# Linear attention and a top-2 mixture of experts on one core: nine tokens a partition for two batches at a time, row-tiled attention matmuls, all of attention and dispatch ahead of the experts

## The chip, the cores and the metric

One core of a Trainium2 chip. The metric is the device time of one execution in microseconds (us), lower is better. Before the change: 599.88 us, median of 3 runs (597.19 to 603.38). Profiles are of single executions; their spans lie 2 us below the times. The runs fell on several chips; they are called by their numbers (9, 14, 11, 5), and the two traces made first, of the kernel before and of the changed one, are "the traces on record".

## The reference, cut to what matters

```python
# q, k, v: (8 batches, 8 heads, 576 tokens, 64); phi(x) = elu(x) + 1
kv  = einsum('bhsd,bhse->bhde', phi(k), v);  z = sum(phi(k), axis=2)
num = einsum('bhsd,bhde->bhse', phi(q), kv); den = phi(q) . z + 1e-6
x   = (num / den), heads side by side                       # (4608 tokens, 512)
noisy = x @ w_gate + log1p(exp(x @ w_noise)) * noise        # (4608, 8)
top2, softmax over the two
for e in range(8):                                          # w1: (8, 512, 1024), w2: (8, 1024, 512)
    for k in range(2):
        out[mask] += top2_w[mask, k] * (relu(x[mask] @ w1[e]) @ w2[e])
```

## The kernel before

Attention runs in four groups of two batches. A group makes kv, then num (which carries the router's logits along in extra columns), then the routing, then 18 indirect scatters ("a dispatch") that put each token's row, with its id and gate, into the list of its expert in DRAM. An expert then takes 1280 rows in three chunks (512, 512, 256): two matmuls, and for each 128 rows a scatter of y into the output. Since a token has two experts, the second one gathers what the first wrote (L), adds and scatters. All of these transfers are issued by GpSimd (POOL), and so are q, k, v and the weights, which are cast on the way; only x, the expert's sorted rows, is loaded by SyncE, transposed on the way.

```python
# load: 4 tokens a partition for 512 tokens of a batch; the last 64 tokens of each batch apart
nc.gpsimd.dma_start(out=kt[:], in_=main(self.k, b))                       # rows of 512 B in bf16
nc.gpsimd.dma_start(out=km[64*j:64*j+64], in_=self.k[b, :, 512:S, :]...)  # rows of 128 B
...
# kv, per batch: 4 full matmuls and one of 64 rows for each pair of heads
for ci in range(4):
    nc.tensor.matmul(out=ps[:, i, 0:192], lhsT=phk[:, hp, ci, :], rhs=vt[:, hp::4, 64*ci:64*ci+64], ...)
nc.tensor.matmul(out=ps[:, i, 0:192], lhsT=phkm[po:po+64, hp, 0, :], rhs=vm[po:po+64, hp::4, :], ...)
...
# experts: weights three ahead, ten gathers at once, x in four buffers
for e in range(E):
    for n in (512, 512, 256):
        xt = self.xp.tile(...)                       # pool of 4
        nc.sync.dma_start(out=xt, in_=x_sorted rows, transpose=True)
        hT = self.mm1(w1, xt, n)
        flush(prev)                                  # mm2, y, scatter of the chunk before
        if t0 == 0:
            if e + 3 < E: self.load_w(e + 3)
            for t in range(T_CAP): L[t] = self.gather(gi[:, t:t+1]) if e > 0 else None
```

Of the kernel before, what the change touches and what calls it, by code (L numbers as in the profile page):

```python
# [15 lines left out]
P = 128  # L16
# [6 lines left out]
NG = 4  # L23
NC = 9
T_CAP = 10
CAP = T_CAP * P
REGION = N_TOK
ROW_W = HD + 16
BIG = 1.0e6
KVW = 162  # L30

# [6 lines left out]
def build_constants(ctx, tc, consts, w_gate, w_noise, noise):  # L38
    nc = tc.nc
    c = {}  # L40

# [19 lines left out]

    c8 = consts.tile([P, E], FP32, name="c8")
    nc.gpsimd.iota(c8[:], pattern=[[-1, E]], base=E, channel_multiplier=0,
                   allow_small_or_imprecise_dtypes=True)
    c["c8"] = c8

    tokid = consts.tile([P, NC], FP32, name="tokid")
    nc.gpsimd.iota(tokid[:, 0:8], pattern=[[S, 2], [1, 4]], base=0, channel_multiplier=4,
                   allow_small_or_imprecise_dtypes=True)
    for half in range(2):  # L70
        nc.gpsimd.iota(tokid[64 * half : 64 * half + 64, 8:9], pattern=[[0, 1]],
                       base=512 + S * half, channel_multiplier=1,
                       allow_small_or_imprecise_dtypes=True)
# [14 lines left out]

    wst = consts.tile([P, 4, 16], FP32, name="wst")
# [11 lines left out]

    noise_sb = consts.tile([P, NG, NC, E], FP32, name="noise_sb")
    for b in range(B):
        g, j = divmod(b, 2)
        nc.scalar.dma_start(
            out=noise_sb[:, g, 4 * j : 4 * j + 4, :],
            in_=noise[b * S : b * S + 512, :].rearrange("(p c) e -> p (c e)", c=4),
        )
    for j in range(2):
        src = noise[512 + j * S : 512 + j * S + 64, :]  # L110
        src = bass.AP(tensor=src.tensor, offset=src.offset,
                      ap=[src.ap[0], [2 * S * E, NG], [1, E]])
        nc.scalar.dma_start(out=noise_sb[64 * j : 64 * j + 64, :, 8, :], in_=src)
# [4 lines left out]
    c["carry"] = carry  # L118
    return c


class PhaseA:
    def __init__(self, ctx, tc, q, k, v, x_sorted, c):
        self.tc, self.nc, self.c = tc, tc.nc, c
        self.q, self.k, self.v, self.x_sorted = q, k, v, x_sorted
        nc = tc.nc
        pool = lambda name, bufs, **kw: ctx.enter_context(tc.tile_pool(name=name, bufs=bufs, **kw))
        self.ld = pool("A_ld", 3)
        self.mx = pool("A_mx", 2)
        self.pers = pool("A_pers", 1)  # L130
        self.tmp = pool("A_tmp", 2)
        self.php = pool("A_php", 2)
        self.kvp = pool("A_kvp", 3)
        self.pq = pool("A_pq", 3)
        self.rt = pool("A_rt", 2)
        self.ps_kv = pool("A_ps_kv", 2, space=PSUM)
        self.ps_t = pool("A_ps_t", 2, space=PSUM)
        self.ps_num = pool("A_ps_num", 2, space=PSUM)
        self.vt = []
        for i in range(4):  # L140
            t = self.pers.tile([P, 12, 256], BF16, name=f"v{i}")
            nc.vector.memset(t[:, 8:12, :], 1.0)
            self.vt.append(t)
        self.vm = []
        for i in range(2):
            t = self.pers.tile([P, 12, D], BF16, name=f"vm{i}")
            nc.vector.memset(t[:, 8:12, :], 1.0)
            self.vm.append(t)
        self.xrow = []
        for i in range(2):  # L150
            t = self.pers.tile([P, NC, ROW_W], BF16, name=f"xrow{i}")
            nc.vector.memset(t[:, :, HD:ROW_W], 0.0)
            self.xrow.append(t)

    def load(self, g):
        nc = self.nc
        st = {"g": g, "k": [], "q": [], "v": []}
        km = self.mx.tile([P, 8, D], BF16, name="km")
        qm = self.mx.tile([P, 8, D], BF16, name="qm")
        vm = self.vm[g % 2]  # L160
        main = lambda t, b: t[b, :, 0:512, :].rearrange("h (p c) d -> p h (c d)", c=4)
        for j in range(2):
            b = 2 * g + j
            kt = self.ld.tile([P, 8, 256], BF16, name="kt")
            qt = self.ld.tile([P, 8, 256], BF16, name="qt")
            vt = self.vt[b % 4]
            nc.gpsimd.dma_start(out=kt[:], in_=main(self.k, b))
            nc.gpsimd.dma_start(out=km[64 * j : 64 * j + 64], in_=self.k[b, :, 512:S, :].rearrange("h p d -> p h d"))
            nc.gpsimd.dma_start(out=vt[:, 0:8, :], in_=main(self.v, b))
            nc.gpsimd.dma_start(out=vm[64 * j : 64 * j + 64, 0:8, :], in_=self.v[b, :, 512:S, :].rearrange("h p d -> p h d"))  # L170
            nc.gpsimd.dma_start(out=qt[:], in_=main(self.q, b))
            nc.gpsimd.dma_start(out=qm[64 * j : 64 * j + 64], in_=self.q[b, :, 512:S, :].rearrange("h p d -> p h d"))
            st["k"].append(kt); st["q"].append(qt); st["v"].append(vt)
        st["km"], st["qm"], st["vm"] = km, qm, vm
        return st

    def phi(self, src, nc_, name):

        nc = self.nc
        n = 512 * nc_  # L180
        flat = src[:].rearrange("p a b -> p (a b)")
        e = self.tmp.tile([P, n], BF16, name=f"e{nc_}")
        t = self.tmp.tile([P, n], BF16, name=f"t{nc_}")
        r = self.php.tile([P, 4, nc_, P], BF16, name=name)
        nc.scalar.activation(out=e[:], in_=flat, func=ACT.Exp)  # L185
        nc.vector.tensor_scalar(out=t[:], in0=flat, scalar1=0.0, scalar2=1.0, op0=ALU.max, op1=ALU.add)
        half = n // 2
        for two in range(2):
            v = lambda x: x[:, half * two : half * two + half].rearrange("p (h c d) -> p h c d", h=4, d=D)
            nc.vector.tensor_tensor(out=r[:, :, :, 64 * two : 64 * two + 64], in0=v(e), in1=v(t), op=ALU.min)  # L190
        return r

    def kv(self, st, j, phk, phkm):
        nc, c = self.nc, self.c
        kvbd = self.kvp.tile([P, 4, KVW], BF16, name="kvbd")
        vt, vm = st["v"][j], st["vm"]
        po = 64 * j
        for half in range(2):
            ps = self.ps_kv.tile([P, 2, 256], FP32, name="kv_ps")
            for i in range(2):  # L200
                hp = 2 * half + i
                for ci in range(4):
                    nc.tensor.matmul(  # L203
                        out=ps[:, i, 0:192],
                        lhsT=phk[:, hp, ci, :],
                        rhs=vt[:, hp::4, 64 * ci : 64 * ci + 64],
                        start=(i == 0 and ci == 0), stop=False, skip_group_check=True,
                    )
                nc.tensor.matmul(
                    out=ps[:, i, 0:192],  # L210
                    lhsT=phkm[po : po + 64, hp, 0, :],
                    rhs=vm[po : po + 64, hp::4, :],
                    start=False, stop=(i == 1), skip_group_check=True,
                )
            nc.vector.tensor_tensor(
                out=kvbd[:, 2 * half : 2 * half + 2, 0:130],
                in0=ps[:, :, 0:130],
                in1=_ap(c["mask"], [[0, 2], [1, 130]]),
                op=ALU.mult,
            )  # L220
        tp = self.ps_t.tile([P, 1024], BF16, name="t_ps")
        for hp in range(4):
            nc.tensor.transpose(tp[:, hp * P : hp * P + P], kvbd[:, hp, 0:128], c["ident"][:])
        kvt = self.kvp.tile([P, 512], BF16, name="kvt")
        nc.scalar.copy(out=kvt[:], in_=tp[:, 0:512])
        wp = self.ps_kv.tile([P, 2, 256], FP32, name="kv_ps")
        wpv = wp[:].rearrange("p a b -> p (a b)")[:, 0:128].rearrange("p (a b) -> p a b", a=4)
        for hp in range(4):
            nc.tensor.matmul(
                out=wpv[:, hp, :], lhsT=kvt[:, hp * P : hp * P + P], rhs=c["wblk"][:, hp, :],  # L230
                start=(hp == 0), stop=(hp == 3), skip_group_check=True,
            )
        nc.vector.tensor_copy(out=kvbd[:, :, 130:162], in_=wpv)
        return kvbd

    def q_t(self, phq):

        nc, c = self.nc, self.c
        pqt = self.pq.tile([P, 4, 512], BF16, name="pqt")
        for half in range(2):  # L240
            tp = self.ps_t.tile([P, 1024], BF16, name="t_ps")
            for i in range(2):
# [8 lines left out]
    def q_tm(self, phqm):  # L251
# [3 lines left out]
        for hp in range(4):  # L255
            nc.tensor.transpose(tp[:, hp * P : hp * P + P], phqm[:, hp, 0, :], c["ident"][:])
# [127 lines left out]
    def run(self):  # L384
        nxt = self.load(0)
        for g in range(NG):
            st = nxt
            if g + 1 < NG:
                nxt = self.load(g + 1)
# [242 lines left out]
```

## Time and profile before

Time 599.88 us, span of the profile 595.4. Milestones, read from the timelines of POOL and TensorE:

| milestone of the kernel before | us |
|---|---|
| matmuls that make the ranks of the four groups (a token's place in its expert's list) | 71.9, 127.4, 171.3, 218.3 |
| last dispatch issued | 243.7 |
| last dispatch landed, first x asked for | 246.0 |
| end | 595.4 |

Read it as four stretches: up to the end of dispatch, from there to the first gather (expert 0, which has none), six periods from one expert's first gather to the next, and the rest. The prediction below shows the lines, and gives the starts of the dispatches and the first gathers.

### The profile page before, as it was taken

What the parts mean: (1) busy time and instruction counts of PE and PEld (TensorE: products, weight loads), DVE (VectorE), ACT (ScalarE), POOL (GpSimd) and SP (SyncE); (2) the same over time, 40 slices, a digit from 0 to 9 for tenths busy, and PEclk for the clock granted to TensorE, in tenths of its full rate; (3) what the DMA queues carried; (4) which work ended last, traced back from release to release, by engine and by line L of the source; (5) the groups of instructions that cost most, each with busy time, mean ns of one, the idle gap of its engine ahead of it and who ended that gap; (6) DMA issues with size and microseconds to landing.
All of it is one profiled execution on the core that took longest, in us unless ns stands there. A gap on an engine that the chain in (4) does not pass through costs nothing. (4 is left out here: it accounts for less than half of the span.)

```text
span 595.4 us, 5833 instructions
## 1 busy us (share of the span) xinstructions
PE 373.5 (63%) x1976; PEld 194.5 (33%) x1976; DVE 221.8 (37%) x638; ACT 170.2 (29%) x265; POOL 288.7 (48%) x315
## 2 busy tenths in 40 slices
PE   0173173137245300199989928969948968989984
PEld 0151142015124100045444404425424434444442
DVE  4359655375650560413233104314304304333122
ACT  0466444025021120062333401421511321423410
POOL 6445378427427117204346516725706726565364
PEclk9996555556555555589999978998987998998998
DMA  9999954995602002555864993993893995573153
GB/s 168 210 191 191 191 131 101 192 209 157 124 27 102 36 10 106 128 91 130 184 101 121 184 110 80 228 140 101 217 120 101 243 146 145 189 157 145 57 160 128
DMA packets 122985, 82.65 MB, mean 139 GB/s; under 512 B 74164, under 2 KB 108980, under 8 KB 122944
## 3 DMA queue, kind: packets, MB, share of 16 engines
q0 software_dynamic: 65888, 69.02, 56.8%
q1 hardware_dynamic: 54272, 12.98, 14.8%
q10 hardware_dynamic: 2784, 0.18, 0.4%
q8 instruction: 17, 0.28, 0.2%
q14 instruction: 24, 0.20, 0.1%
HBM read 80.72 MB, written 32.87 MB: 191 GB/s over the span
## 5 line engine op out<-in xcount | busy, mean ns | idle before, releaser
L474 PE MATMUL h_ps<-xt,w 128*128 128x512 bf16 (+1 forms) x768 | 150.5, 355 | 39.5 <-DMA xt<-x_sorted 32.3
L476 ACT ACTIVATE hT<-h_ps 128x512 bf16<-128x512 f32 (+1 forms) x192 | 99.4, 527 | 260.8 <-PE h_ps L474 209.2
L483 PE MATMUL y_ps<-w,hT 128*128 128x512 bf16 x640 | 149.8, 392 | 36.5 <-DVE y L489 36.5
L490 POOL DMA_INDIRECT out_dram<-y,si x80 | 79.4, 992 | 97.4 <-DVE y L487 39.9
L474 PEld LDWEIGHTS <-w 128*128 128x128 bf16 x768 | 77.8, 101 | 111.1 <-issue 46.9
L376 POOL DMA_INDIRECT x_sorted<-xrow,posi x72 | 73.6, 1022 | 78.9 <-DVE xrow L373 33.7
L461 POOL DMA_INDIRECT L<-out_dram,gi x70 | 70.6, 1009 | 82.1 <-DMA out_dram<-y,si 60.6
L483 PEld LDWEIGHTS <-hT 128*128 128x128 bf16 x640 | 64.1, 100 | 115.5 <-issue 45.3
L489 DVE SCALAR_TENSOR_TENSOR y<-y_ps,gate,L 128x512 f32<-128x512 f32 x70 | 51.1, 731 | 98.8 <-PE y_ps L483 60.6
L460 DVE MEMSET L<- 128x512 f32 x70 | 34.0, 485 | 34.4 <-DMA x_sorted<-xrow,posi 24.4
L270 PE MATMUL num_ps<-kvbd,pqt 128*128 128x162 bf16 x128 | 22.2, 324 | 38.6 <-DVE lwt L293 34.6
L203 PE MATMUL kv_ps<-v,phk 128*128 128x192 bf16 x128 | 26.0, 360 | 19.0 <-DVE phk L190 19.0
L335 PE MATMUL kv_ps<-A,ut 128*128 128x72 bf16 x4 | 0.9, 219 | 44.2 <-DVE A L331 44.2
L270 PEld LDWEIGHTS <-pqt 128*128 128x128 bf16 x128 | 13.2, 130 | 45.6 <-DVE lwt L293 41.3
L248 ACT COPY pqt<-t_ps 128x1024 bf16<-128x1024 bf16 x16 | 16.0, 1014 | 32.5 <-PE t_ps L244 10.6
L287 DVE TENSOR_TENSOR xrow<-num_ps,rden 128x512 bf16<-128x512 f32 x36 | 24.7, 687 | 0.5
L444 DVE SCALAR_TENSOR_TENSOR isf<-meta 128x10 f32<-128x10 f32 x8 | 1.4, 174 | 58.5 <-DMA meta<-x_sorted 58.5
L203 PEld LDWEIGHTS <-phk 128*128 128x128 bf16 x128 | 14.1, 131 | 23.6 <-DVE phk L190 19.0
L244 PE MATMUL t_ps<-ident,phq 128*128 128x128 bf16 x128 | 16.0, 306 | 8.0 <-ACT pqt L248 4.5
L185 ACT ACTIVATE e<-kt 128x2048 bf16<-128x2048 bf16 x8 | 15.2, 1912 | 10.7 <-DMA kt<-in_k_dram 7.9
L487 DVE TENSOR_SCALAR y<-y_ps,gate 128x512 f32<-128x512 f32 x10 | 7.5, 750 | 28.7 <-PE y_ps L483 28.7
L244 PEld LDWEIGHTS <-phq 128*128 128x128 bf16 x128 | 13.7, 144 | 9.2 <-issue 9.2
(116 smaller groups left out, 277.2 us busy)
## 6 DMA issues: line engine op xcount, KB each, us to landing
w<-in_moe_w_dram POOLq DMA_DIRECT2D x32, 512.0 KB
kt<-in_k_dram POOLq DMA_DIRECT2D x8, 512.0 KB
v<-in_v_dram POOLq DMA_DIRECT2D x8, 512.0 KB
qt<-in_q_dram POOLq DMA_DIRECT2D x8, 512.0 KB
x_sorted<-zrow SPq DMA_DIRECT2D x8, 264.0 KB, 6.6
out_dram<-y,si POOLq DMA_INDIRECT x80
x_sorted<-xrow,posi POOLq DMA_INDIRECT x72
L<-out_dram,gi POOLq DMA_INDIRECT x70
```

The costliest lines, as they stand in the source:

```text
L203: nc.tensor.matmul(out=ps[:, i, 0:192], lhsT=phk[:, hp, ci, :], rhs=vt[:, hp::4, 64 * ci : 64 * ci + 64], start=(i == 0 and ci == 0), stop ...
L244: nc.tensor.transpose(tp[:, i * 512 + ci * P : i * 512 + ci * P + P], phq[:, 2 * half + i, ci, :], c["ident"][:],)
L270: nc.tensor.matmul(out=ps[:, hp, 0:KVW], lhsT=pqs[j][:, hp, cc * P : cc * P + P], rhs=kvbds[j][:, hp, :], start=(hp % 2 == 0), stop=(hp % ...
L287: nc.vector.tensor_tensor(out=_ap(xrow[:, ci, 0:HD], [[64, 4], [256, 2], [1, 64]]), in0=_ap(ps, [[256, 4], [64, 2], [1, 64]]), in1=_ap(rd, ...
L376: r = nc.gpsimd.indirect_dma_start(out=self.x_sorted, out_offset=bass.IndirectOffsetOnAxis(ap=posi[:, ci, sl : sl + 1], axis=0), in_=xrow[ ...
L460: nc.vector.memset(L[:], 0.0)
L461: nc.gpsimd.indirect_dma_start(out=L[:].bitcast(INT32), out_offset=None, in_=self.out.bitcast(INT32), in_offset=bass.IndirectOffsetOnAxis( ...
L474: nc.tensor.matmul(out=ps[:, 0:n], lhsT=w1[:, dc, fc * P : fc * P + P], rhs=xt[:, dc, 0:n], start=(dc == 0), stop=(dc == 3))
L476: nc.scalar.activation(out=hT[:, fc, 0:n], in_=ps[:, 0:n], func=ACT.Relu)
L483: nc.tensor.matmul(out=ps[:], lhsT=hT[:, fc, t * P : t * P + P], rhs=w2[:, fc, :], start=(fc == 0), stop=(fc == 7))
L489: nc.vector.scalar_tensor_tensor(out=y[:], in0=ps[:], scalar=gate, in1=L[:], op0=ALU.mult, op1=ALU.add)
L490: r = nc.gpsimd.indirect_dma_start(out=self.out, out_offset=bass.IndirectOffsetOnAxis(ap=si, axis=0), in_=y[:], in_offset=None, bounds_che ...
```

## The change

It is meant to shorten attention: each partition takes nine tokens of one batch (batch j of the pair on partitions 64j to 64j+63), so that tail tiles go and rows grow to 1152 B; kv becomes pairs of matmuls over 64 rows that can run side by side; num and its small columns are split so that VectorE works on three chunks at a time; one activation table serves all. All experts then follow.

```diff
+    nc.scalar.preload_act_table_set(ACT_SET)
 def load(self, g):
-    ... 12 transfers: kt, km, vt, vm, qt, qm for each of two batches
+    for t in "kvq":
+        x = self.vt[g % 2] if t == "v" else self.kq.tile([P, 8, S], BF16, name="kq")
+        for j in range(2):
+            self.last_load = nc.gpsimd.dma_start(out=x[64*j : 64*j+64, 0:8, :],
+                in_=getattr(self, t)[2*g + j].rearrange("h (p c) d -> p h (c d)", c=9)).ins
 def kv(...):
-    for ci in range(4): matmul over 128 rows;  one matmul over 64 rows
+    for ci in range(9):
+        for j in range(2):
+            half = slice(64*j, 64*j + 64)
+            nc.tensor.matmul(out=ps[j][:, i, 0:192], lhsT=phk[half, hp, ci, :],
+                             rhs=vt[half, hp::4, 64*ci : 64*ci+64], ...)
 def route(...):
-    nc.vector.tensor_scalar_add(out=fld(0), in0=c["tokid"][:], scalar1=float(g * 2 * S))
+    nc.scalar.activation(out=fld(0).bitcast(INT32), in_=c["tokid"][:, c0:c1], func=ACT.Copy, bias=...)
 class PhaseB:
-    self.xp = pool("B_x", 4); L in 12 buffers; three weight buffers
+    self.xp = pool("B_x", 2); L in 3 + 5 buffers; weights in 3 + 4 buffers
 def expert(...):
-    flush(prev) after mm1; all ten gathers in the first chunk
+    tails of the chunk before between the parts of mm1
+    for t in range(t0, t0 + n // P):
+        L[t] = self.gather(gi[:, t : t + 1])          # this chunk's only
 # after attention
-    weights: load_w(e + 3) inside expert e
+    for e in range(E1, 5):
+        pb.load_w(e, 1)                               # experts 3 and 4 (5, 6, 7 follow in the loop)
```

## The prediction

> **What bounds the kernel now.** I read the table of stages first (busy time of each engine per stretch, cut where the trace showed the first and last dispatch, the first expert matmul and the gathers), because whole-span shares mix two programs.
>
> ```profile
> core 0: us, PE busy (x) PEld busy (x) DVE busy (x) ACT busy (x) POOL busy (x), PEclk, DMA share, GB/s
> 0.00:60.00 60.00, 19.07 (x132) 12.70 (x133) 35.37 (x96) 25.86 (x21) 30.36 (x49) 0.90 1.42 190
> 100.00:130.30 30.30, 5.80 (x44) 3.67 (x44) 15.73 (x63) 3.94 (x6) 12.16 (x17) 0.50 1.24 188
> 174.10:197.00 22.90, 12.17 (x85) 8.19 (x84) 1.99 (x6) 3.10 (x4) 17.43 (x18) 0.50 0.28 101
> 221.20:243.80 22.60, 0.00 (x0) 0.00 (x0) 0.02 (x1) 0.00 (x0) 17.32 (x18) 0.50 0.28 102
> ```
>
> Up to 130 us the transfers are full (q, k, v and the weights of two to three experts, 190 GB/s); after it they are idle and the time is a chain. Attention runs in four groups of two batches. Group g is: kv, num, route, then a dispatch of 18 scatters on the POOL queue. The dispatches start at 74.7, 130.3, 174.1 and 221.2 us (timeline); one that nothing holds up takes 22.6 us (last line: DVE, ACT and PE are idle during it). The first expert matmul starts at 251.1. So attention is 246 us, then 5 us for the first x.
>
> The experts I read from the POOL timeline, since gathers and scatters share that queue:
>
> ```profile
> 476.85 1.04 POOL L490 DMA_INDIRECT out_dram<-y,si  x1 [0.30 <-DMA out_dram<-y,si]
> 488.27 1.07 POOL L461 DMA_INDIRECT L<-out_dram,gi  x1 [10.37 <-DMA out_dram<-y,si]
> 489.65 1.01 POOL L461 DMA_INDIRECT L<-out_dram,gi  x1 [0.31 <-issue]
> ...
> 558.23 0.97 POOL L490 DMA_INDIRECT out_dram<-y,si  x1 [0.75 <-DVE y L489]
> 561.59 1.05 POOL L461 DMA_INDIRECT L<-out_dram,gi  x1 [2.39 <-DMA out_dram<-y,si]
> ...
> 573.42 1.00 POOL L461 DMA_INDIRECT L<-out_dram,gi  x1 [0.30 <-issue]
> 576.90 1.02 POOL L490 DMA_INDIRECT out_dram<-y,si  x1 [2.48 <-issue]
> 578.23 1.00 POOL L490 DMA_INDIRECT out_dram<-y,si  x1 [0.30 <-issue]
> ```
>
> Read: the ten gathers of an expert wait until every earlier scatter has landed, and its scatters wait until every gather has. A turn costs 2.4 us on a quiet queue (561.59, 576.90), but 10.4 to 16.1 us where a weight load stands ahead of the last scatter (488.27). First gathers stand at 305.8, 354.3, 397.4, 445.1, 488.3, 522.1 and 561.6: periods of 48.5, 43.1, 47.6, 43.2 with a weight load inside, 33.9 and 39.5 without. PE needs 34.6 us an expert (32 x 512 columns take 6.91 us in the chain; twice that, half of it, and ten y tiles of 1.73). These rows say who waited:
>
> ```profile
> L461 POOL DMA_INDIRECT L<-out_dram,gi x70 | 70.6, 1009 | 82.1 <-DMA out_dram<-y,si 60.6
> L376 POOL DMA_INDIRECT x_sorted<-xrow,posi x72 | 73.6, 1022 | 78.9 <-DVE xrow L373 33.7
> L335 PE MATMUL kv_ps<-A,ut 128*128 128x72 bf16 x4 | 0.9, 219 | 44.2 <-DVE A L331 44.2
> L483 PE MATMUL y_ps<-w,hT 128*128 128x512 bf16 x640 | 149.8, 392 | 36.5 <-DVE y L489 36.5
> L270 PE MATMUL num_ps<-kvbd,pqt 128*128 128x162 bf16 x128 | 22.2, 324 | 38.6 <-DVE lwt L293 34.6
> ```
>
> Gathers idled 60.6 us for scatters; PE idled 44.2 us for route's vector chain, 34.6 for num's evacuation and 36.5 for y. The kernel is a latency chain with PE 63% busy.
>
> **What the Trainium skill says.** "TensorEngine Tiling (Array Packing)", Key Properties: tiles of the array run load and matmul independently; and Instruction Overhead: about 60 cycles a matmul whatever its width. The trace agrees for column tiles: the ninth chunk's eight half-width matmuls (162 columns) took 0.75 us, as four whole ones do. "DMA: Bandwidth & Descriptors", Anatomy of one DMA: about 2.0 us fixed per transfer, most of it the write receipt; the 2.4 us turns agree. The same page, Specifications: below 512 B a packet loses rate; the page of before counts 74,164 of 122,985 packets below it, and pure weight loads (1 and 2 KB rows) ran at 205 to 215 GB/s against 191 for q, k, v. "ScalarE: Activation LUTs", What ACT_TABLE_LOAD costs: 1283 ns, with Exp and Ln in one set; the trace has seven loads in route of 1283 ns each.
>
> **The change, part by part.** I read it from the diff and from the order and waits of the built program.
>
> (a) Nine tokens a partition. The 48 loads of q, k, v become 24 with rows of 1152 B instead of 512 and 128. I take 210 GB/s, so 14.2 MB take 68 us instead of 74. The separate tail tiles go, and with them eight small phi operations per group.
>
> (b) DVE per group. Durations scale from the rows (t 2048 elements 0.73, 512 0.33; min 1024 0.68, 256 0.28): phi 4.1 us each for k and q; masks 4 x 0.43; num now 9 x 0.69 + 3 x (0.17 + 0.20 + 0.55) = 8.9 instead of 9 x 1.32 = 11.9; reduce 2.1; route 6. About 27 us instead of some 31 (125 us by four, with waits of neighbours). Route also loses one table load of 1.28 on its path.
>
> (c) PE per group: kv is 72 half-row matmuls instead of 40; as concurrent pairs 36 x 0.205 = 7.4 us (14 if they do not pair). 44 transposes 5.7, num as 36 narrow plus 36 wide pairs 9.3. From one group's rank matmuls to the next: kv with two evacuations 9.5, its transform 3.5, num 15, reduce to rank 6.3: 34 us. Before, that period was 47.0 for the last group (171.3 to 218.3).
>
> (d) The POOL order. Dispatch 0 stands behind the loads of group 2; dispatch 1 behind experts 1 and 2's weights and group 3. Eight transfers can be in flight, so a dispatch's first eight scatters wait for those loads. Bytes up to the end of dispatch 1: 20.5 MB of loads at 210 (98 us), the zero rows (now after group 0's num) and two dispatches at about 380 (20 us), 4 us of start, and some 18 us in which dispatch 0 keeps the loads out: 140 us (before: 154.6).
>
> (e) From there it is a chain. On ACT, group 2's softplus stands behind the token-id write of group 3's rows, which waits for dispatch 1: rank at 144. One period of 34 gives 178, 2 to the positions, 22.8 of dispatch, 2 to land: T = 206, against 246. Gain 40.
>
> (f) Experts. Loads of experts 3 to 7 are now all issued at T in a new pool, ahead of and between expert 0's scatters: 10 MB at 210 (48 us), 2.6 MB of scatters (7), 2.4 MB of x (at its uncontended rate 10), so its last scatter lands, and expert 1's first gather goes, at T + 62 (before T + 60, with PE as the limit).
>
> (g) Experts 1 to 7. Gathers now come by chunk (4, 4, 2), and in the built order each chunk's gathers wait for the previous chunk's scatters and the reverse: three turns each way per expert instead of one. A chunk of four: gathers 3 x 1.307 + 1.0 = 4.9, turn 2.4, scatters 3 x 1.28 + 1.0 = 4.8, turn 2.3: 14.4. A chunk of two: 9.3. Sum 38.1, so PE's 34.6 is no longer the limit; POOL is. The weight loads' 10 to 16 us turns are gone. The interleaving keeps y tiles ready: PE gets two tiles ahead (y_ps alternates a pool of one buffer with one of three) and the fourth is done about 1 us before its scatter's turn. Six periods are 230 against 255.8: gain 26, of which (f) takes back 2.
>
> (h) End: from expert 7's first gather, 38.1 less the last turn plus the 4.6 us from the last scatter to the end: 40.4, against 33.8.
>
> Sum of the span: 206 + 62 + 230 + 40.4 = 538. The timed runs lie 2 to 8 us above the span of 595.4, so 542.
>
> **The rivals.**
> 1. The new turns eat the gain: if a turn costs 3.5 us because x transposes are in flight, an expert takes 45 and the second half gains nothing: 580. For it: contended turns of 7 us and more occur in before. Against it: nine quiet turns, with x traffic around, were 2.2 to 3.0.
> 2. Attention stays DMA- and dispatch-bound: if the larger rows bring nothing (190 GB/s) and row pairs do not overlap, rank 2 comes at 155 and the last period is 40: T = 223, 558 in all. For it: halves of a tile are loaded by two transfers, and PE's granted clock is 0.5 there. Against: weight rows of like size ran faster.
> 3. The burst at T hurts more: x loads share the engines with 10 MB of weights (up to 12.5 us to land in before), so expert 0 needs 80 us: 560.
> 4. Better than thought: the last period 28 and G(e1) at T + 50: 520.
>
> **Range and chances.** Rivals 2 and 3 are each fairly likely in part and rival 1 unlikely in full; together they give 520 to 572. Anything under 588 is faster by 2%. Getting there needs both rival 1 whole and half of rival 2. Faster 0.95, same 0.04, slower 0.01.
>
> **What would show each step.** (a) GB/s near 210 in the first 60 us; (b) num's group near 3 us per three chunks on DVE; (c) pairs of kv matmuls starting within 0.1 us; (d, e) last dispatch starting near 181 and the first expert matmul near 211, with ACT idle before a token-id write; no table load after the first; (f) first gather some 62 us after the last dispatch landed, with POOL waiting on weight loads; (g) gathers in runs of 4, 4, 2 with an idle of 2.2 to 2.6 us before each run and each scatter run, period 38, PE waiting on y each chunk; (h) end 40 us after the last expert's first gather. The prediction is wrong if a period exceeds 42, if the first expert matmul comes after 228, or if PE rather than POOL paces the experts.

## The result, and the profile after

The changed kernel took 630.48 us (median of 4 runs, 627.33 to 631.83) against 600.27: ratio 1.0496, 95% interval 1.0427 to 1.0564. Ratios here are the mean time of one kernel's runs over that of the other's of the same rounds, so not quite the ratio of the medians that stand beside them. Executions over 1.5% slower than the fastest of the same kernel are left out of the means. It is slower by 5%, where 10% faster was predicted, outside the range.

| stretch | before | after, predicted | after, measured |
|---|---|---|---|
| to the landing of the last dispatch (x or a weight load starts) | 246.0 | 206 | 228.3 |
| to the first gather of expert 1 | 59.8 | 62 | 95.1 |
| six periods | 255.8 (42.6 each) | 230 (38.3) | 252.4 (42.1) |
| from the last expert's first gather to the end | 33.8 | 40.4 | 54.2 |
| span | 595.4 | 538 | 630.0 |

So attention did gain 18 us, and the experts lost 52. The table of stages of the changed kernel (columns: stretch, its length, busy time of the five engines with counts, granted clock, DMA engines' share, GB/s):

```profile
core 0: us, PE busy (x) PEld busy (x) DVE busy (x) ACT busy (x) POOL busy (x), PEclk, DMA share, GB/s
0.00:60.00 60.00, 18.37 (x302) 15.71 (x303) 39.67 (x84) 24.72 (x22) 17.10 (x33) 0.80 1.13 203
155.80:178.30 22.50, 7.90 (x81) 6.45 (x77) 1.53 (x4) 1.39 (x2) 17.30 (x18) 0.50 0.31 111
178.30:203.50 25.20, 9.53 (x174) 7.73 (x175) 16.53 (x54) 5.48 (x9) 0.00 (x0) 0.57 0.02 7
228.30:323.40 95.10, 54.41 (x222) 23.77 (x222) 11.69 (x33) 18.60 (x34) 25.18 (x30) 0.74 1.13 162
```

The loads run at 203 GB/s (190 before). Beside dispatch 2 (second line) VectorE and ScalarE do almost nothing, and the last group's work falls into the third line, with the DMA engines idle. The last line is expert 0: 95 us with the DMA engines full and TensorE busy for 54. Two causes in attention show in ScalarE's timeline (start, length, then idle time before it and what ended it):

```profile
148.56 0.22 ACT L340 ACTIVATE xr<-tokid 128x9 int32<-128x9 f32 x1 [20.69 <-DMA x_sorted<-xr,posi]
148.68 0.25 ACT L286 ACTIVATE sp<-lg 128x72 f32<-128x72 f32 x1
...
167.12 1.01 ACT L205 COPY kvt<-misc 128x1024 bf16<-128x1024 bf16 x1 [14.90 <-remote]
171.40 0.37 ACT L212 CAST kvbd<-misc 128x256 bf16<-128x256 f32 x1 [3.27 <-remote]
179.83 1.01 ACT L225 COPY pqt<-misc 128x1024 bf16<-128x1024 bf16 x1 [8.05 <-remote]
181.28 1.01 ACT L225 COPY pqt<-misc 128x1024 bf16<-128x1024 bf16 x1 [0.44 <-remote]
```

First, group 2's softplus (second line) stood behind a token-id write that waited for dispatch 1 to land, although its logits were ready at 136.8: 12 us. Second, in the last group the copies waited for TensorE's signals ("remote": the signal came when no instruction that gives it had just ended). The transposes that line 179.83 waits for stand at 168.42 to 169.43 in TensorE's timeline; going by each signal and the matmul that ended last before it, six signals came 2 to 8.4 us late between 162 and 182. The kernel before has the same in its last group, from 190.7 to 199.5.

In the experts, TensorE's waits for x (start, length, and in brackets the idle time) show where expert 0 lost its time, and the costliest groups (busy, mean ns, idle time and its main cause) show the rest:

```profile
244.93 8.53 PE L450 MATMUL h_ps<-xt,w 128*128 128x512 bf16 x32 [43.72 <-DMA xt<-x_sorted]
262.56 3.59 PE L450 MATMUL h_ps<-xt,w 128*128 128x512 bf16 x8 [9.10 <-DMA xt<-x_sorted]
300.54 3.57 PE L450 MATMUL h_ps<-xt,w 128*128 128x512 bf16 x8 [10.73 <-DMA xt<-x_sorted]
317.94 3.59 PE L450 MATMUL h_ps<-xt,w 128*128 128x512 bf16 x8 [4.23 <-DMA xt<-x_sorted]
```

```profile
L450 PE MATMUL h_ps<-xt,w 128*128 128x512 bf16 (+1 forms) x768 | 159.1, 355 | 67.8 <-DMA xt<-x_sorted 67.8
L458 PE MATMUL y_ps<-w,hT 128*128 128x512 bf16 x640 | 167.1, 409 | 33.2 <-DVE y L464 33.0
L438 POOL DMA_INDIRECT L<-out_dram,gi x70 | 71.4, 1020 | 85.2 <-DMA out_dram<-y,si 66.5
L309 PE MATMUL misc<-A,ut 128*128 128x72 bf16 x4 | 0.9, 217 | 44.6 <-DVE A L305 44.6
```

Gathers idled 66.5 us for scatters, where before it was 60.6: not in six waits but in twenty. One chunk of four in POOL's timeline (575.79 is the first gather of expert 7):

```profile
575.79 1.04 POOL L438 DMA_INDIRECT L<-out_dram,gi  x1 [3.52 <-DMA out_dram<-y,si]
...
584.25 1.02 POOL L465 DMA_INDIRECT out_dram<-y,si  x1 [3.48 <-DVE L L435]
...
591.64 1.04 POOL L438 DMA_INDIRECT L<-out_dram,gi  x1 [2.53 <-DMA out_dram<-y,si]
```

It is built as predicted (4, 4, 2 with a turn each way), but the turns are longer. Over the experts 1 to 7, 21 turns from gather to scatter take 2.85 us on average and 20 from scatter to gather 3.10, from 1.91 to 4.82; 2.4 and 2.3 were predicted. At the end, POOL's closing drain takes (min/median/max in ns, kernel before first):

```profile
L627 POOLq DRAIN  x3: 46/103/1048, 593.5 to 595.2; - x3
```

```profile
L665 POOLq DRAIN  x3: 46/103/8317, 620.9 to 629.8; - x3
```

8.3 us instead of 1.0, with every other engine done.

### The profile page after: what moved, and what is told of

Read it like the earlier page. It is cut to its first block, busy times and chain, and to the rows that moved or that the text cites. A ratio compares the mean times of both kernels' runs of the same rounds, so it can differ in the third digit from the quotient of the medians.

```text
span 630.0 us, 6653 instructions
## 1 busy us (share of the span) xinstructions
PE 376.8 (60%) x2520; PEld 204.8 (33%) x2520; DVE 204.0 (32%) x449; ACT 162.1 (26%) x257; POOL 265.9 (42%) x289
## 5 line engine op out<-in xcount | busy, mean ns | idle before, releaser
L458 PE MATMUL y_ps<-w,hT 128*128 128x512 bf16 x640 | 167.1, 409 | 33.2 <-DVE y L464 33.0
L358 POOL DMA_INDIRECT x_sorted<-xr,posi x72 | 72.8, 1011 | 84.0 <-issue 51.4
L438 POOL DMA_INDIRECT L<-out_dram,gi x70 | 71.4, 1020 | 85.2 <-DMA out_dram<-y,si 66.5
L458 PEld LDWEIGHTS <-hT 128*128 128x128 bf16 x640 | 66.5, 104 | 115.5 <-issue 55.5
L435 DVE MEMSET L<- 128x512 f32 x70 | 34.0, 485 | 34.2 <-DMA x_sorted<-xr,posi 24.5
L173 ACT ACTIVATE e<-kq 128x2304 bf16<-128x2304 bf16 x16 | 33.5, 2122 | 27.6 <-PE misc L191 8.6
L191 PE MATMUL misc<-v,e 64*128 64x192 bf16 x288 | 24.4, 330 | 21.6 <-DVE e L177 19.9
L240 PE MATMUL num<-kvbd,pqt 128*64 128x128 bf16 x288 | 20.4, 283 | 26.4 <-DVE xr L259 25.9
L240 PEld LDWEIGHTS <-pqt 128*64 128x64 bf16 x576 | 21.8, 144 | 42.3 <-DVE xr L259 24.5
L191 PEld LDWEIGHTS <-e 64*128 64x128 bf16 x288 | 20.7, 123 | 24.1 <-DVE e L177 19.9
L259 DVE TENSOR_TENSOR xr<-num,rden 128x512 bf16<-128x512 f32 x36 | 23.5, 686 | 2.7 <-PE num L240 1.8
L225 ACT COPY pqt<-misc 128x1024 bf16<-128x1024 bf16 (+1 forms) x20 | 17.9, 932 | 17.2 <-remote 8.5
L177 DVE TENSOR_TENSOR e<-e,kq 128x2304 bf16<-128x2304 bf16 x16 | 21.3, 1342 | 0.1
```

What stands on the lines that cost most here:

```text
L173: nc.scalar.activation(out=ev(two), in_=xv(two), func=ACT.Exp)
L191: nc.tensor.matmul(out=ps[j][:, i, 0:192], lhsT=phk[half, hp, ci, :], rhs=vt[half, hp::4, 64 * ci : 64 * ci + 64], start=(i == 0 and ci == ...
L240: nc.tensor.matmul(out=out[half], lhsT=pqt[ci][:, hp, half], rhs=kvbd[:, j, hp, cols], start=start, stop=stop, skip_group_check=True)
L259: nc.vector.tensor_tensor(out=_ap(xr[:, ci, 0:HD], [[64, 4], [256, 2], [1, 64]]), in0=_ap(ps, [[128, 4], [64, 2], [1, 64]]), in1=_ap(rden[ ...
L358: r = nc.gpsimd.indirect_dma_start(out=self.x_sorted, out_offset=bass.IndirectOffsetOnAxis(ap=posi[:, ci - c0, sl : sl + 1], axis=0), in_= ...
L435: nc.vector.memset(L[:], 0.0)
```

## The experiments

**Theories.** Mine: three separate causes, the turns (periods; a turn is the wait between gathers and scatters of one expert, either way), the burst of weights when attention ends (expert 0) and the token-id write (dispatch 2), with the late signals as a thing of their own that the kernel before has too. Rivals: two x buffers instead of four; y buffers; dispatches that slow TensorE. The control of the runs on chip 9 is e13, the changed kernel itself: 620.2 us, span 618.3. It was made in a later session than e1 to e4; e4, of the first session, turned out to be another control, with 614.7 us, so differences of some 5 us between runs on chip 9 say nothing.

### e1: gathers and scatters of one expert independent

```diff
+        self.tc.declare_no_dep(r.ins, group=f"sc{e}", reason="rows of one expert are distinct")   # each gather
+        self.tc.add_to_no_dep_group(f"ga{e}", r.ins)
+            tc.declare_no_dep(r.ins, group=f"ga{e}", reason="rows of one expert are distinct")    # each scatter
+            tc.add_to_no_dep_group(f"sc{e}", r.ins)
```

> The changed kernel, with the gathers and scatters of one and the same expert declared independent (their rows are distinct), so that only the first gathers of an expert wait for the expert before. Theory 'turns': the three turns each way per expert are what holds the period at 42.1 us; with one turn left it falls to 35 to 37, six periods to some 218 instead of 252, the end by some 6, and the time from 630 to about 590. Rival 'y buffers or x': the period stays at 40 or more and the time at 615 or more.

Measured (chip 9): correct, 555.4 us against 587.1 of the kernel before, ratio 0.9516 (0.9413 to 0.962). The periods are 36.0, 33.7, 34.8, 34.3, 35.5, 34.2; from the control the six fall from 253.8 to 208.4 and the end from 54.3 to 41.5. TensorE never waits for y any more:

```profile
L461 PE MATMUL y_ps<-w,hT 128*128 128x512 bf16 x640 | 153.0, 383 | 0.0
```

More than expected: the turns not only lengthened POOL's round but kept y from TensorE. A period is now about TensorE's own 34.6 us, so neither y buffers nor x, the rivals, held it.

### e2: no weight loads for experts 3 to 7 (wrong result)

```diff
-    for e in range(E1, 5):
-        pb.load_w(e, 1)
+    for e in range(E1, E):
+        pb.w[e] = pb.w[e % E1]
-        if e in (2, 3): pb.load_w(e + 3, 1)
-        if e == 4: pb.load_w(7)
```

> The changed kernel without the weight loads of experts 3 to 7: they compute with the weights of experts 0 to 2 again (a wrong result on purpose). Theory 'burst': the 10 MB issued when attention ends hold back x and the scatters of expert 0, so the stretch from the end of the last dispatch (228) to the first gather falls from 95 us to 55 to 65, the time to about 597, and the later periods stay at 42. Rival 'two x buffers and the queue order': the stretch stays above 80, the time above 615.

Measured (chip 9): 566.0 us, span 564.2 against 618.3. From the last dispatch's issue to the first gather 54.7 us (209.1 to 263.8) against 99.8 in the control; the periods stay at 40.5 to 43.6. After the first x, TensorE does not wait for x again:

```profile
216.81 11.68 PE L450 MATMUL h_ps<-xt,w 128*128 128x512 bf16 x40 [32.61 <-DMA xt<-x_sorted]
```

The burst costs 45 us (42 against e4, where the stretch is 96.3). Its 20 pieces are 10.5 MB; at the 200 GB/s that the engines moved from 240 to 260 us of the changed kernel's trace they take some 52 us (an estimate from these two numbers). So most of the burst was added to the 54.7 us that expert 0 needs without it, and little of it passed beside. Not every piece goes out when attention ends: in the trace on record twelve do (228.3 to 247.5), and eight stand between the scatters (274.6 to 315.2). I read the loss as a chain, x, then y, then the next x into a freed buffer, in which every link waits behind weights; that reading is not shown apart from the engines simply being full, which they were for nearly the whole stretch. Of the other 9 us that this run gains on the control, 6.6 are at the end (47.7 instead of 54.3), 5.2 of them the closing drain.

### e3: the token-id write behind softplus

```diff
-        nc.scalar.activation(out=sp, in_=sp, func=ACT.Ln, bias=1.0, scale=1.0)
+        ln = nc.scalar.activation(out=sp, in_=sp, func=ACT.Ln, bias=1.0, scale=1.0).ins
+        with tc.issue_after(ln):
             nc.scalar.activation(out=fld(0).bitcast(INT32), in_=c["tokid"][:, c0:c1], func=ACT.Copy, ...)
```

> The changed kernel, with ScalarE's token-id write issued behind softplus instead of ahead of it. Theory: group 2's softplus no longer waits 12 us for dispatch 1 to land; dispatch 2 starts at 147 to 149 instead of 155.8, right behind dispatch 1; the last dispatch then starts 8 to 12 us earlier (192 to 196) and the time is about 620. Rival: what is won is lost in the last group, because TensorE's results come late as long as dispatches run: last dispatch after 200, time 628 or more.

Measured (chip 9): 599.7 us, span 597.8 against 618.3. The third rank matmul stands at 141.1 instead of 152.8, dispatch 2 starts at 147.7 right behind dispatch 1, the last one at 172.7 instead of 187.9. The theory holds for dispatch 2 (7.9 us earlier); 3.4 of the last dispatch's 15.2 us are a shorter last period (28.8 us instead of 32.2). The absolute 192 to 196 was read off the traces on record and does not fit this chip.

### e4: dispatch 2 held back, which failed

```diff
+                nc.gpsimd.tensor_copy(out=hd[:], in_=pa.lwt[:, 8, 7])   # waits for the last group's num
+                pa.dispatch()                                            # the scatters of group 2
```

> The changed kernel, with dispatch 2 held back until the last group's num is done (a small copy on the POOL queue waits for it), so that no scatter runs beside the last group. Theory 'dispatch disturbs TensorE': the matmuls' signals, up to 8 us late in the last group, are on time again; from the third rank matmul to the fourth 34 to 38 us instead of 47.7, and the time is some 6 to 10 us longer only (one more dispatch of 22.8 on the path, 10 to 13 saved). Rival 'the matmuls are late by themselves (half clock, row tiles)': 46 to 48 us between the ranks and the time 20 us longer.

Measured (chip 9): 614.7 us, dispatch 2 at 155.6 as ever. The scheduler had put the copy behind the scatters (it ran at 178.06), so nothing was held and the run is one more control. It showed something else: 31.4 us between the last ranks and no late signal, with the dispatch running beside. So did e1 to e3.

### e5 and e6: both kernels again, on chip 14

> The kernel before, unchanged, for a second trace of it. On the chip of the first traces, matmul signals came up to 8.6 us late in the last attention group of both kernels; on the chip of the runs e1 to e4 none came more than 1.5 us late. Theory 'that lateness belongs to the chip or to the run, not to the change': a trace without it has 30 to 35 us between the third and the fourth rank matmul instead of 47.0, and the time is 580 to 588; the experts' periods stay 34 to 48. Rival: 47 again, whatever the lateness.

> The changed kernel, unchanged, as the control on this chip. Expected: 1.045 to 1.055 of the kernel before, whether or not the last group has late signals, since both kernels have them or have them not; the stretch from the last dispatch's end to the first gather 92 to 97 us, periods 41 to 43 and some 13 us from the last scatter to the end.

Measured: before 583.6 us (span 581.8), 33.7 us between the last ranks instead of 47.0 and no late signal in attention; after 615.9, ratio 1.0492 (1.0416 to 1.0568), 29.8 us instead of 47.7. So in that period the traces with late signals are 13 us longer in the kernel before and 18 in the changed one, and the ratio hardly differs (1.0496 and 1.0492). One expectation was missed by a little: the periods of before were to be 34 to 48 and are 34.2 to 49.6. From before to after on this chip: attention 21.4 less (229.2 to 207.8 for the last issue), expert 0 39.2 more (60.3 to 99.5), periods 11.3 less (260.4 to 249.1), end 23.0 more (31.9 to 54.9): 29.5 more.

### e7: the three mends together

```diff
+    def piece(self, e, k, behind): ...              # 512 KB of w1 or w2, issued behind a given scatter or gather
+            c0 = t0 // 4 - (e == 0)
+            if e < 5 and 0 <= c0 < 2:
+                for k in (2 * c0, 2 * c0 + 1):
+                    self.piece(e + 3, k, self.last_pool)
     (and the edits of e1 and e3; no load_w after attention)
```

> The changed kernel with three mends: gathers and scatters of one expert independent, the token-id write behind softplus, and the weights of experts 3 to 7 loaded in 512 KB pieces, two at a time, one expert ahead of another by three, instead of in a burst when attention ends. If the three causes are separate they add up: from the control, some 15 (dispatch 2 at once behind dispatch 1), 41 (burst; 53 us from the last dispatch to the first gather) and 43 to 50 (periods of 35): 110 less, some 505, or 0.86 of the kernel before. If they overlap (PE then waits for x or weights): over 530.

Measured (chip 14): correct, 523.9 us, ratio 0.8888 (0.8826 to 0.895). The profiled run counts as slow (528.8 us); e15, the same kernel with a fast profile, has the same picture (58.2, 37.3 to 41.3, then 35.7 and 34.3). The stretch to the first gather is 56.0 us and dispatch 2 starts at 148.5, as the parts did; but the periods with a weight piece in them are 37.7 to 42.3, and only the last two, without, 36.6 and 34.3. The time lies between the two expectations (505, or over 530). So the causes are separate except for the weights, which now cost in the periods some of what they cost in the burst. TensorE's row says what it waits for (some 32 us of it is the wait ahead of the first x, as in e2, and the rest stands inside the experts):

```profile
L469 PE MATMUL h_ps<-xt,w 128*128 128x512 bf16 (+1 forms) x753 | 156.7, 352 | 46.7 <-DMA xt<-x_sorted 44.8
```

### e8: four x buffers in the changed kernel

```diff
+    pb.xp.append(right("B_x2", 2))        # and x takes the two pools in turn
```

> The changed kernel with four x buffers from the end of attention on instead of two, as the kernel before had. Rival to 'burst' that runs e2 left open: x comes late since its load waits for a free buffer and then stands behind the weights. If that is most of it, the stretch to the first gather falls from 94 to 75 or less and the time by 20 or more; if the weights' bytes themselves are the limit, it stays above 85 and the time within 8 of the control.

Measured (chip 14): 606.7 us, span 604.9 against 611.3; the stretch 89.8 us against 99.5. Under the burst, two buffers instead of four cost some 10 us of expert 0 and 6 of the whole; without it they cost nothing that shows, since e2 has two and needs 54.7. The rival is a small part. What was expected had a stretch above 85 as the sign that the weights' bytes themselves are the limit, and the DMA engines are as full as in the control (share 1.11 at 181 GB/s against 1.12 at 156). That speaks for full engines at least as much as for the chain that I read into e2.

### e9: ten gathers at once, all waits kept

```diff
-                for t in range(t0, t0 + n // P):
+            if t0 == 0:                          # in the expert's first chunk
+                for t in range(nt):
                     L[t] = self.gather(gi[:, t : t + 1])
-    right("B_l2", 5)
+    right("B_l2", 9)
```

> The changed kernel with the ten gathers of an expert issued together, as the kernel before had them (nine late L buffers instead of five so that they find room), and every wait between gathers and scatters kept. It tells whether the count of turns is what counts or the independence that e1 declared. Theory 'turns': one turn each way per expert, and no weight load in it any more, gives the 34 us that the kernel before shows in its two periods without a load; the time is 40 to 55 below the changed kernel's 612 to 630. Rival (the chunks overlap with the work, and ten gathers at once hold TensorE up): periods of 40 or more.

Measured (chip 11): 581.8 us, span 580.0; the control on that chip, e17, has 619.8. Periods 37.0, 38.1, 37.2, 36.6, 39.4 and 44.5, six turns from scatter to gather at 2.25 on average. The gathers' row shows where the change of turns went: the wait for scatters, 66.5 us in the changed kernel, is 14.3 here (four times), less than the gathers' own issue.

```profile
L438 POOL DMA_INDIRECT L<-out_dram,gi x70 | 70.3, 1005 | 40.8 <-issue 25.0
```

The whole gives back 40 us, at the edge of what was expected, but the periods missed: 34 was expected, and one of them is above 40. By stretches against e17 it is 23 us in the six periods (256.1 to 232.8), 9 at the end, 6 before the first gather and 1 in attention. In the periods e1 gained 45, so the count of turns is about half of that. I put the rest down to an expert's first scatter no longer waiting for its last gather; no run shows that by itself. The run also has twelve L buffers instead of eight, which was not tried alone.

### e10 and e11: more x buffers and smaller pieces on top of e7

> The kernel of e7 with four x buffers in the experts instead of two. In e7 TensorE idled 45 us for x, part of it in the middle of the experts, where x stood behind a weight piece; with x loaded two chunks earlier that goes, the periods with a weight load in them (37.7 to 42.3) fall to 35 to 36, and the time from 524 to 500 to 512, 0.85 to 0.87 of the kernel before. If the weight pieces hold back the last scatters instead, the periods stay near 40 and the time above 515.

Measured (chip 11): 522.3 us, ratio 0.8861 (0.8767 to 0.8956), as e7. The wait for x is gone, but periods with a piece are still 38.5 to 41.2: TensorE now waits for y, whose L was gathered behind two pieces.

```profile
354.98 3.51 PE L477 MATMUL y_ps<-w,hT 128*128 128x512 bf16 x8 [4.57 <-DVE y L483]
```

The expectation was missed: the wait moved. e11 issued each piece by itself (behind gathers 4, 6, 8 and 10):

> The kernel of e10 with each 512 KB weight piece by itself (behind gathers 4, 6, 8 and 10 of an expert) instead of two at a time. In e10 TensorE no longer waited for x but up to 4.6 us at a time for y, whose L had been gathered behind two weight pieces, and the periods with a load in them were 38.5 to 41.2 against 33.6 and 34.0 without. If two pieces at a time are what delays L, the periods fall to 36 to 37 and the time from 522 to 508 to 514 (0.87 of the kernel before). If the last pieces now stand ahead of an expert's last scatters and delay the turn to the next, the periods stay at 38 or more and the time within 5 of e10.

Measured (chip 5): 580.1 us, ratio 0.9665. Not comparable: here signals came late again, one by 29.5 us (matmuls issued by 144.65, signal at 174.51, two dispatches running from 115.6 to 170.3), 61.3 us between the last ranks. Periods of 38.6 to 45.1.

### e12: does the closing drain follow the number of transfers?

```diff
+        for i in range(20):                      # near the start
+            nc.gpsimd.dma_start(out=sc[:], in_=moe_noise[0:1152, :]...)
```

> The changed kernel with 20 small transfers more (36 KB each, into a tile that nobody reads) on the POOL queue near the start, where that queue waits anyway. POOL's closing drain took 1.05 us in the kernel before (302 transfers on its queue) and 8.32 in the changed one (278), 3.09 in e2 (258). If its length follows the number of transfers on the queue, it changes (to some 13 us, or to a small value if it wraps); if it is set by something else, it stays 8.32. The rest of the time should move by less than 5 us.

Measured (chip 5): 644.0 us, drain 8.56. With 20 transfers more it moved by 0.24 us, so the count does not set it. The condition on the rest failed: the small transfers stood ahead of loads and put dispatch 0 from 65.6 to 80.9, and the signals were late again.

### e13 to e18: late signals, and the pieces side by side

e14 and e18 are e4 with the scatters ordered behind the copy (`with tc.issue_after(cp)`), e13 and e17 their controls; e15 is e7, e16 is e11.

> The changed kernel, unchanged, as the control on this chip. If the chip is one with late signals: 46 us or more between the third and the fourth rank matmul and a time near 630; if not, 28 to 32 and a time near 613.

> The changed kernel with dispatch 2 kept back until the last group's num is done, this time with its scatters ordered behind the copy that waits. On a chip with late signals: if the dispatch delays TensorE, the fourth rank matmul follows the third by 28 to 34 us, no signal of that group is over 1.5 us late, and the time is 8 to 16 us longer than the control (dispatches 2 and 3 then follow one another, 45 us from some 182 on, against 203.5 + 22.6); if it does not, 46 or more and late signals again. On a chip without them: 28 to 34 as in the control, and the time some 20 longer.

> The kernel of e7 again, on another chip and beside e16. Expected 0.88 to 0.90 of the kernel before on a chip without late signals, 0.90 to 0.94 on one with them (30 us may be lost, as in e11), periods 37 to 42 with a weight load in them.

> The kernel of e11 (one weight piece at a time, four x buffers) beside e15. If one piece at a time is worse, as the periods of 38.6 to 45.1 in e11 say against 38.5 to 41.2 in e10, its six periods sum to over 240 here too, against 233 in e7; if those were the chip, they sum to 225 to 235.

> The changed kernel, unchanged, as the control. On a chip with late signals 46 us or more between the third and the fourth rank matmul and some 630 in all; otherwise 28 to 33 and 611 to 620.

> Dispatch 2 kept back until the last group's num is done, as in e14. On a chip with late signals, if the dispatch delays them: 28 to 34 us between the ranks, none over 1.5 us late in the last group, and a time 2 to 12 us over the control or under it; if something else delays them: 46 or more. On a chip without late signals: as e14, some 10 us over the control, and the question stays open.

Measured: on chip 9 e13 620.2, e14 630.4; on chip 11 e17 621.6, e18 629.6. This time dispatch 2 was held (179.0 and 176.9), yet neither chip has late signals, and the ranks stand 31.6 and 29.9 us apart against 32.3 and 32.2. On such chips a dispatch beside the last group costs it 0.6 to 2.3 us at most; whether it delays the signals on the others stays open. (e14 is 10 us longer than its control, where 20 were expected; e18 8, where 10 were.) ScalarE's lines of e13, which answer to those above, show the last group without lateness: these waits come to 11.0 us instead of 26.7, close to the 15.5 us by which the period is shorter:

```profile
162.02 1.01 ACT L205 COPY kvt<-misc 128x1024 bf16<-128x1024 bf16 x1 [10.01 <-PE misc L203]
163.52 0.37 ACT L212 CAST kvbd<-misc 128x256 bf16<-128x256 f32 x1 [0.49 <-PE misc L208]
164.37 1.93 ACT L225 COPY pqt<-misc 128x1024 bf16<-128x1024 bf16 x2 [0.48 <-PE misc L224]
```

e15: 524.0 us against 587.4, ratio 0.9028 (0.8966 to 0.909). The ratio is higher than that of the medians (0.892) since four of the seven runs of before on that chip counted as slow. e16: 527.2 us, six periods 231.9 (253.1 to 485.0) against 228.6 in e15. One piece at a time is no better, and not much worse: so most of e11's 253.8 came with its chip, and that two pieces stand together is not what keeps the periods of e10 near 39. What does stays open. e15's 0.9028 is just above what was expected of it, and the record calls this comparison unclear.

A version that beats both kernels is therefore e7 (e15, and e10 with them): 522 to 524 us, 0.89 to 0.90 of the kernel before on chips without late signals; e11, at 0.9665 on a chip with them, is the only one of that family measured there.

## Why the prediction was right or wrong

Against the kernel before I had put 40 less, 2 more, 26 less, 7 more; it came to 18 less, 35 more, 3 less, 20 more (in the order of the table above).

- **Reading of the bound: right.** A latency chain on the POOL queue and the routing: e1, e2, e3, e8 and e9 each shortened a wait in it and the kernel with it; e10 only moved one. One line was read too simply: up to 130 us the transfers of the kernel before were not full throughout, since beside dispatch 0 (74 to 104 us) the page has the DMA engines at 0.5 and 0.4.
- **(a), (b), (c): right.** 203 GB/s for 210; VectorE takes 2.9 us for three chunks of num (3.0); 72 matmuls over 64 rows take 3.59 + 3.37 = 7.0 us (7.4), so the pairs overlap. One table load is left, ahead of everything (that Exp and Ln are in one set stands in another section of the page that the prediction names, on table sets). None of it set the time.
- **(d): right in kind, 9 us short.** The third rank came at 153.0, not 144. Dispatch 0 kept loads off the queue for 25 us (65.6 to 90.6), not 18, and the rate was 203. The wait of softplus for the token-id write was named as it came; e3 shows that without it the third rank comes 12 us earlier.
- **(e): the period of 34 us was undercut on three chips (28.5 to 32.3) and passed in the trace on record.** There it was 47.7, where the same kernel has 29.8 to 32.3 without late signals (e6, e13, e17), so 15 to 18 us of it came with them. The step that failed is "Before, that period was 47.0": I took all of it for work that the change shortens, where some 13 us were late signals (33.7 in e5) that no part of the change touches. The terms of (e) also add to 205, not 206.
- **(f): the largest miss, 33 us; without it the two kernels would have been level (597). The step that failed is the overlap.** I counted expert 0 as transfers that line up once (48 + 7 + 10 us, which add to 65 and were put down as 62), with TensorE's work beside them. The bytes were right: the engines moved 15.4 MB in the stretch, and I had 15.0. But they took 95 us at 162 GB/s, and on chip 9 the burst's 45 us came on top of the 54.7 that expert 0 needs without it (e2, against 99.8 in e13). TensorE stood for x 16.7 us at first (asked for at 228.2), then 9.1, 10.7 and 4.2 more: 40.7, of which 5 to 6 are a first x that nothing delays (5.1 in the kernel before, 5.6 in e2). And the first sixteen matmuls after each of the three later waits took 8 us more in all than they do elsewhere (3.59 and 3.11 at 262.56, against 1.89 for eight). Together that is some 43 of the 45. Whether the links waited in turn or the full engines were just slower than I had put them, no run separates. Rival 3 named this and sized it at 80; it was 95. The loss is the change's own: both kernels have the weights of three experts by then, but the kernel before asks for four x tiles first and issues its next weight load at 278.6, 33 us after the first x, one expert at a time.
- **(g): the mechanism right, the turn mis-sized.** 38.1 becomes, with turns of 2.85 and 3.10 instead of 2.4 and 2.3, 38.1 + 3 x (0.45 + 0.8) = 41.9; measured 42.1. The turns I took it from were in stretches with one turn an expert. This was rival 1, held unlikely in full; it took the whole gain of the second half but 3 us. e1 shows that the turns together with the independence are worth 45 us in the periods, e9 that the count of turns alone is worth 23.
- **(h): 14 us short, two thirds of it a wait of which nothing in the profile before spoke.** A third (4.7 us) is the last expert's longer round: its last scatter was issued 40.5 us after its first gather, against 38.1 - 2.3 = 35.8. From there to the end 13.7 us passed instead of 4.6, 7.3 of the 9.1 more in POOL's closing drain. What sets the drain stays open; it belongs to the program and not to the run, for all eleven runs with the changed kernel's transfers have 8.317 or 8.318 us, whatever the chip.

Two of the three tests named for "wrong" fired: first expert matmul after 228 (244.9), periods over 42. What misled was treating the four terms as independent and each at its quiet value: the chance of "slower" was 0.01 because I let the rivals differ one at a time, and several came together: rival 1 in part (periods of 42.1, where it had 45), rival 3 and more, with the drain on top. Rival 2's T of 223 was passed too (228.3), but not for its reasons, since the rate was 203 and the pairs overlapped.

## What to carry to other kernels

When a change moves all of a phase's loads to its end, do not take them to pass beside the work that follows: list what that work has to send over the same engines while they drain. Here 42 to 45 of some 52 us were simply added. When a dependency on one tensor alternates two kinds of transfers, count the turns: each cost 3 us here, and issuing the ten gathers in three groups cost 40 us (e9), about twice what the faster attention gained. Before crediting a change with shortening a stretch, look whether its waits end on something the change touches.

## What the Trainium skill lacked or had wrong

- "DMA: Bandwidth & Descriptors", Anatomy of one DMA, gives a fixed part of about 2.0 us that scales with nothing; with the page's term for the bytes that makes some 2.6 us for the 256 KB of a gather or scatter here (an estimate from its formula). The turns, from the last issue of one kind to the first of the next, took 2.85 and 3.10 us on average, but from 1.91 to 4.82 for one size. The page's own section Latency and other measured facts does say that the fixed cost falls with lighter load on HBM. What no page has is a figure for a transfer that shares the engines with a burst of loads: the first x took 16.7 us beside it and 5.6 without (e2).
- "Perfetto Trace Analysis", Tensor Engine Instruction, says that a matmul's end in the profile is an estimate and that its semaphore is given after it. The traces agree, but in the traces on record and on chip 5 signals came 2 to 29.5 us after that end, all of them in attention for matmuls beside a running dispatch, and on chips 9, 14 and 11 none in attention came more than 1.5 us late. No page says when that happens.
- No page has a drain of POOL at the end of a kernel that takes microseconds; the drains that pages speak of are VectorE's own and short ones that the runtime adds. Here it took 1.05 us in the kernel before, 8.32 in the changed one on all chips, 3.09 without 20 of its weight loads (e2), 7.34 with the loads spread (e7), 8.56 with 20 transfers more (e12).
